# Rows of q and k loaded in three pieces, with gaps in the row buffers

## The chip, the core and the metric

The kernel runs on one core of a Trainium2 chip. The core has five engines that run their own instruction streams and wait for each other on semaphores: TensorE (matmuls, with its weight loads shown apart), VectorE (DVE), ScalarE (ACT), GpSimd (POOL) and SyncE (SP). Sixteen DMA engines move data between the chip's main memory and the two on-chip memories' buffer side (SBUF); matmul results go to eight PSUM banks of 128 x 512 float32. The metric is the device time of one execution in microseconds (us), as a median over runs. Lower is better.

## What is computed

Attention over 64 heads (8 batches of 8), each with 576 rows of 64 values, followed by a feed-forward layer. Each head's output is the sum of a coarse attention, over means of four rows, and a local attention, over rows at most three apart:

```python
q_d = q.reshape(B, H, Sd, factor, D).mean(axis=3)
...
out_d = sm_attn(q_d, k_d, v_d)
out_up = np.repeat(out_d, factor, axis=2)
mask = np.abs(pos[:, None] - pos[None, :]) < factor
...
out_local = np.matmul(attn, v)
return (out_up + out_local).astype(np.float32)
...
h = x @ w_in
g = h * (1.0 / (1.0 + np.exp(-h)))
return (g @ w_out).astype(np.float32)
```

`x` has one row for each of the 4608 positions and 512 columns (8 heads of 64); `w_in` is 512 x 2048, `w_out` 2048 x 512.

## The kernel before

The heads are handled as 32 pairs. One pair's q is a block of memory of 2 x 576 x 64 float32; the kernel reads it as 128 rows of 576 contiguous values, one row to a partition (9 positions of 64 values each). The same holds for k, whose blocks are read 64 rows further on, so that one k block serves two pairs in halves.

For pair 0, q and k come as float32 through the queues of SP and ACT, and VectorE and ScalarE convert them to bf16 into the buffer `qkb` (L753, L759). For pairs 1 to 31, POOL issues two DMAs a pair (q and k, L686; the issue itself is recorded at L676 or L740) that convert float32 to bf16 on the way and write `qkb` directly. `qkb` has six buffers of 128 x 2 x 576 bf16; a buffer is free again when TensorE has transposed what is in it and the next pair's half. These DMAs all go through one queue, q0, in the order in which POOL issues them. The eight blocks of the weights, `w_in` and `w_out`, go through the same queue, in between (L740, 512 pieces of 2048 B read for each block). The rows of v go through SP's queue, q1, in packets of 256 B (`vs`) and of 1024 B (`vq`), the outputs in packets of 2048 B.

TensorE transposes each pair's q and k in 36 small steps: a step takes 64 partitions and 64 values of a row (`pe_T`, L802, instructions at L810). The results are copied to `qT` and `kT`, from which the scores are formed (L571, "PS<-qT,kT"); exponentials, sums and products with v follow, and POOL's add at L1018 writes the result of a pair, transposed, into `xT`. Four pairs make one batch's 576 positions. The feed-forward layer runs in nine super blocks of 512 positions: 16 groups of four matmuls "PS<-xT,w_in_sb" each, ScalarE and VectorE in between, and then 16 matmuls "PS<-w_out_bf,gT" for each of four output tiles. Super block j can start only when the adds of all pairs that it covers are done: super block 0 needs pairs 0 to 3, super block 1 pairs 4 to 7 too, and so on. Until TensorE has such work it fills gaps with dummy matmuls on a constant ("PS<-dz").

The order of all instructions on every engine is fixed when the program is built, by a planner (class `Plan`, L253) that steps through a model of the engines with the cost written beside each job. The costs of the loads (0.87 and 0.57, `gran=0.106`, L688) are not touched by the change, so the order that comes out is the same instruction by instruction on all five engines; only line numbers and the shapes of the changed operands differ. POOL runs its stream strictly in order: row DMAs, weight DMAs, conversions of v (L565, "vb<-vs"), sums over four rows of v (L785, L790), and the adds (L1018).

The branch in `casts` that would convert a pair's q and k on POOL (L771) is never taken here, since the set `SW` holds all pairs from 1 to 31.

Of the kernel before, what the change touches and what calls it, by code (L numbers as in the profile page):

```python
# [6 lines left out]
AF = mybir.ActivationFunctionType  # L7
# [3 lines left out]
BF16 = mybir.dt.bfloat16  # L11
# [37 lines left out]
def D(p, left):  # L49
    return (22 + 1.5 * (p - 3) if p < 4 else 42 + 3 * (p - 7) if p < 8 else 45 + 8 * (p - 7)) - left  # L50
# [37 lines left out]
def HOLD(p):  # L88
    return ["S3"] if p == 4 else []
# [405 lines left out]
def bass_hourglass_attn__then__act_silu_kernel(  # L495
# [9 lines left out]
    with kctx:  # L505
        E = kctx.enter_context
        L = Plan()
        P = Prog()
        J = L.job
        res = {}  # L510

        def R(name, psum=False):
            if name not in res:
                res[name] = Res(name, psum)
            return res[name]

        def sb(name, shape, dt, n=None):
            if n is None:
                return E(nc.sbuf_tensor(name, shape, dt))
            return [E(nc.sbuf_tensor(f"{name}{i}", shape, dt)) for i in range(n)]  # L520
# [10 lines left out]
        vs = sb("vs", [128, 10, 64], F32, N_VS)  # L531
        vq = sb("vq", [128, 4, 256], F32, N_VQ)
        vt = sb("vt", [128, 4, 128], F32)
        qkb = sb("qkb", [128, 2, 576], BF16, N_QKB)
        vb = sb("vb", [128, 10, 64], BF16, N_VB)
        vd = sb("vd", [128, 4, 64], BF16, N_VD)
        qT = sb("qT", [128, S_], BF16, N_T)
# [26 lines left out]
        def copy(eng, e, out_, in_):  # L564
            return e.activation(out_, in_, AF.Copy) if eng == "ACT" else e.tensor_copy(out_, in_)  # L565

        def half(j):
            return slice(64 * j, 64 * j + 64)
# [102 lines left out]
        def rows(t, p, n, off):  # L671
            return bass.AP(tensor=t.tensor, offset=t.offset + (128 * p + off) * 576, ap=[[576, n], [1, 576]])

        def dma(name, eng, out_, in_, r, w, sem, work, cost, hold=(), **kw):
            def emit(j):
                P.op(j.ran, lambda s: s.dma_start(out_(), in_()), r() if r else [], w(), sem(), after=gates(hold))  # L676
            kw["pre"] = list(kw.get("pre", ())) + list(hold)
            J(name, eng, cost, emit, work=work, **kw)

        def loads(p, order):  # L680
            if p == 0:
                dma("lkx", LD_ENG("kx", 0), lambda: kx[64:128, :], lambda: rows(k, 0, 64, 0), None, lambda: rkx, lambda: "kx",
                    0.45, 0.43, due=order["kx"], take=[("qkb", -1)])
            for x, (t, n, off) in enumerate(((q, 128, 0), (k, 128 if p < NPAIR - 1 else 64, 64))):
                if p in SW:
                    dma(f"c{'qk'[x]}{p}", "POOL", lambda x=x, n=n: qkb[S("qkb", p)][0:n, x, :],  # L686
                        lambda t=t, n=n, off=off: rows(t, p, n, off), None, lambda x=x: [R(f"qkb{S('qkb', p)}{x}")],
                        lambda x=x: f"qkb{S('qkb', p)}{x}", 0.87, 0.57, gran=0.106, take=[("qkb", p)], due=-60 + p if p < 4 else D(p, 26.0),  # L688
                        hold=order.get(("gate", p), ()))
                    continue  # L690
                dma(f"l{'qk'[x]}{p}", LD_ENG("qk"[x], p), lambda x=x, n=n: qk[S("qk", p)][0:n, x, :],
                    lambda t=t, n=n, off=off: rows(t, p, n, off), None, lambda x=x: [R(f"qk{S('qk', p)}{x}")],
                    lambda x=x: f"qk{S('qk', p)}{x}", 0.85 * n / 128, 0.43, take=[("qk", p)] + ([("qkb", 0)] if p == 0 else []), due=order["qk", p],
                    hold=order.get(("gate", p), ()))
            for h in range(2):
                for j in range(2):
                    def emit(jb, h=h, j=j):
                        s = S("vs", p)
                        sem, w = f"vs{s}{h}{j}", [R(f"vs{s}{h}{j}")]
                        base = v[(2 * p + h) // H_, (2 * p + h) % H_]  # L700
                        T_, o = base.tensor, base.offset + (288 * j - 3) * D_
                        d, lo, hi = vs[s][half(j), 5 * h:5 * h + 5, :], 0, 5
                        if (p, h, j) == (0, 0, 0):
                            lo = 1
                            P.op(jb.ran, lambda e: e.dma_start(vs[s][3:64, 0, :], bass.AP(
                                tensor=T_, offset=base.offset, ap=[[64, 61], [1, 64]])), [], w, sem, after=gates(["vz"] + list(order.get(("gate", p), ()))))
                        if (p, h, j) == (NPAIR - 1, 1, 1):
                            hi = 4
                            P.op(jb.ran, lambda e: e.dma_start(vs[s][64:123, 9, :], bass.AP(
                                tensor=T_, offset=base.offset + 517 * D_, ap=[[64, 59], [1, 64]])), [], w, sem)  # L710
                        P.op(jb.ran, lambda e: e.dma_start(d[:, lo:hi, :], bass.AP(
                            tensor=T_, offset=o + 58 * 64 * lo, ap=[[64, 64], [58 * 64, hi - lo], [1, 64]])), [], w, sem,
                            after=gates(order.get(("gate", p), ())))
                    J(f"lv{p}{h}{j}", LD_ENG("v", p), 0.64, emit, work=0.39, gran=0.018, take=[("vs", p)],
                      due=order["v", p], pre=list(order.get(("gate", p), ())) + (["vz"] if p == 0 else []))
            if p >= VP_PE:
                def emit(jb):
                    i = S("vq", p)
                    base = v[2 * p // H_, 2 * p % H_]
                    T_, o = base.tensor, base.offset  # L720
                    P.op("SP", lambda e: e.dma_start(vq[i][:, 0:4:2, :], bass.AP(
                        tensor=T_, offset=o, ap=[[256, 128], [S_ * D_, 2], [1, 256]])), [], [R(f"vqm{i}")], f"vq{i}")
                    for j in range(2):
                        P.op("SP", lambda e, j=j: e.dma_start(vq[i][64 * j:64 * j + 16, 1:4:2, :], bass.AP(
                            tensor=T_, offset=o + 128 * 256, ap=[[256, 16], [S_ * D_, 2], [1, 256]])),
                            [R(f"vqc{i}1"), R(f"vqc{i}3")], [R(f"vqe{i}{j}")], f"vqe{i}{j}")
                J(f"lvq{p}", "SP", 1.6, emit, work=0.85, gran=0.046, take=[("vq", p)], due=order["vq", p],
                  pre=list(order.get(("gate", p), ())) + [f"vqz{(p - VP_PE) % N_VQ}"])
# [18 lines left out]
        def casts(p):  # L747
# [2 lines left out]

            def one(x):
                def emit(jb):
                    P.op(jb.ran, lambda e, a=i(), b=j(): copy(jb.ran, e, qkb[b][:, x, :], qk[a][:, x, :]),  # L753
                         [R(f"qk{i()}{x}")], [R(f"qkb{j()}{x}")])
                return emit

            if p == 0:
                def emit(jb):
                    P.op("ACT", lambda e, b=S("qkb", -1): e.activation(qkb[b][64:128, 1, :], kx[64:128, :], AF.Copy),  # L759
                         rkx, [R(f"qkb{S('qkb', -1)}1")])  # L760
                J("ckx", "ACT", 0.65, emit, pre=["lkx"], take=[("qkb", -1)], due=D(0, 9.4))
            use = dict(take=[("qkb", p)], use=[("qk", p)])
            if p in SW:
                pass
            elif p < CAST2:
                for x in range(2):
                    eng = C_ENG[p][x]
                    J(f"c{'qk'[x]}{p}", eng, {"DVE": 0.5, "ACT": 0.65, "POOL": 0.6}, one(x), pre=[f"l{'qk'[x]}{p}"],
                      port=True, due=D(p, 9.3), **use)
            else:  # L770
                def emit(jb):  # L771
                    P.op("POOL", lambda e, a=i(), b=j(): e.tensor_copy(qkb[b][:, :, :], qk[a][:, :, :]),
                         [R(f"qk{i()}0"), R(f"qk{i()}1")], [R(f"qkb{j()}0"), R(f"qkb{j()}1")])
                J(f"cq{p}", "POOL", 1.15, emit, pre=[f"lq{p}", f"lk{p}"] + HOLD(p), port=True, due=D(p, 10.3), marks={f"ck{p}": 1.0}, **use)

            def emitv(jb):
                a, b = S("vs", p), S("vb", p)
# [24 lines left out]
        def pe_T(p):  # L802
            a, b = S("qkb", p), S("qkb", p - 1)
            tiles = ((0, 0, 0, a), (0, 1, 1, a), (1, 1, 0, a), (1, 0, 1, b))
            for r in range(9):
                for j, h, x, n in tiles:
                    t, c = t_home(p, x, r)
                    o = PS[half(h), t, c:c + 32].bitcast(BF16)
                    w = qkb[n][half(j), x, 64 * r:64 * r + 64]
                    P.op("PE", lambda e, o=o, w=w, j=j: e.transpose(o, w, idn[half(j), :]),  # L810
                         [R("idn"), R(f"qkb{n}{x}")], [rB[t]])

# [484 lines left out]
```

## Time and profile before

| | |
|---|---|
| median of three runs | 341.86 us (341.33 to 343.66) |
| the profiled execution | 342.31 us, of which the span from first to last instruction is 340.5 us |
| granted TensorE clock over the span | 0.97 |
| busy: TensorE, VectorE, ScalarE, POOL | 96%, 67%, 53%, 46% |
| DMA queue q0 (POOL's): packets, share of 16 engines over the span | 13088, 26.2% |
| DMA queue q1 (SP's): packets, share | 56378, 30.8% |
| row DMAs into `qkb` from q: count, median from issue to landing | 31, 5.0 us |
| row DMAs into `qkb` from k: count, median from issue to landing | 30 of 128 rows, 5.4 us, and one of 64 |

The profile is one execution. The span is cut into 40 slices of about 8.5 us; this is TensorE's busy share, its granted clock and the DMA engines' busy share in each, in tenths:

```profile
PE   5587999999999999999999999999999999999996
...
PEclk9755999999999999999999999999999999999999
DMA  8997879999878976996398339500100010000112
```

The first four slices differ from the rest: TensorE is not full there and its clock is partly at half speed, while the DMA engines are busy. From the fifth slice on TensorE is full, and the DMA engines stay busy until about the 26th.

A duration in the profile is that of the recorded instruction or packet. TensorE's matmuls overlap, so sums of their durations exceed the time that passes. A packet's time includes waiting beside packets of other queues, so the shares of the queues can add up to more than 1. "issue" in the chain of waits is time in which an engine waited for nothing that the profile shows.

### The profile page before, as it was taken

How to read it: one execution, taken by the hardware profiler on the slowest of the kernel's cores; microseconds unless marked ns; L12 is line 12 of the kernel's file. 1: busy time of each engine (PE TensorE's matmuls, PEld its weight loads, DVE VectorE, ACT ScalarE, POOL GpSimd, SP SyncE). 2: the span in 40 equal slices, each digit the busy share in tenths (PEclk: the TensorE clock that was granted, in tenths of full speed). 3: DMA queues.
4: the chain of work that ended last, by engine and by line, in shares of the span. 5: the costliest groups of instructions: out<-in, count | busy, mean ns of one | idle time of the engine just before them, and what ended most of it. 6: DMA issues, size and time to landing. Idle time of an engine off the chain costs nothing.

```text
span 340.5 us, 10780 instructions
## 1 busy us (share of the span) xinstructions
PE 326.8 (96%) x4623; PEld 213.9 (63%) x4623; DVE 229.6 (67%) x410; ACT 179.0 (53%) x317; POOL 156.6 (46%) x211
## 2 busy tenths in 40 slices
PE   5587999999999999999999999999999999999996
PEld 2465677865555775587557755785577558866544
DVE  6586989866667885788577857796767556754200
ACT  5542756665544765476447645664656416644221
POOL 7363498435679667970698068704400140000000
PEclk9755999999999999999999999999999999999999
DMA  8997879999878976996398339500100010000112
GB/s 168 175 252 156 255 181 212 198 229 234 172 178 195 213 177 151 209 202 174 76 240 180 81 57 249 115 1 33 66 31 2 33 64 31 2 1 31 62 64 92
DMA packets 70666, 44.59 MB, mean 131 GB/s; under 512 B 45914, under 2 KB 63770, under 8 KB 70618
## 3 DMA queue, kind: packets, MB, share of 16 engines
q1 hardware_dynamic: 56378, 28.00, 30.8%
q0 software_dynamic: 13088, 15.36, 26.2%
q8 instruction: 36, 0.59, 0.7%
q10 hardware_dynamic: 1152, 0.54, 0.7%
q14 instruction: 12, 0.10, 0.1%
HBM read 45.61 MB, written 9.44 MB: 162 GB/s over the span
## 4 chain that ended last, share of the span: by engine, by line
PE 92%; DMA 2%; DVE 2%; issue 2%; POOL 1%; ACT 0%; POOLq 0%
PE PS L571 89%; PE PS L810 3%; DMA qkb<-in_k_dram 2%; DVE Pt L899 1%; POOL qkb L676 0%; DVE qd L845 0%; POOL gT L601 0%; DVE Rb L974 0%; DVE qT L565 0%; DVE kd L845 0%; DVE zt L964 0%; DVE zr L968 0%; ACT osb L1076 0%; DVE vd L565 0%; POOL idw L610 0%
## 5 line engine op out<-in xcount | busy, mean ns | idle before, releaser
L571 PE MATMUL PS<-xT,w_in_sb 128*128 128x512 f32 x576 | 141.2, 399 | 0.0
L571 PE MATMUL PS<-w_out_bf,gT 128*128 128x512 bf16 (+1 forms) x592 | 131.3, 374 | 0.0
L571 PEld LDWEIGHTS PS<-xT,w_in_sb 128*128 128x128 f32 x576 | 106.7, 188 | 24.7 <-DVE gT L1047 0.7
L1047 DVE SCALAR_TENSOR_TENSOR gT<-th,PS 128x512 bf16<-128x512 f32 x144 | 96.9, 683 | 37.0 <-ACT th L1043 36.3
L1043 ACT ACTIVATE th<-PS 128x512 f32<-128x512 f32 x144 | 86.1, 599 | 54.2 <-PE PS L571 46.0
L571 PEld LDWEIGHTS PS<-w_out_bf,gT 128*128 128x128 bf16 x592 | 54.7, 98 | 62.9 <-issue 3.5
L1018 POOL TENSOR_TENSOR xT<-xo 128x576 fp32r<-128x576 f32 (+5 forms) x48 | 43.5, 919 | 51.5 <-DVE xo L990 51.4
L565 POOL CAST vb<-vs 128x640 bf16<-128x640 f32 x32 | 24.4, 767 | 57.3 <-PE PS L571 42.5
L1100 ACT ACTIVATE osb<-PS 128x512 f32<-128x512 f32 x35 | 21.1, 603 | 53.6 <-PE PS L571 53.6
L893 ACT ACTIVATE Pt<-PS 128x576 bf16<-128x576 f32 x32 | 20.8, 649 | 33.0 <-PE PS L571 32.8
L785 POOL TENSOR_TENSOR vt<-vq 128x512 f32<-128x512 f32 x24 | 30.8, 1285 | 10.0 <-DMA vq<-in_v_dram 9.9
L990 DVE TENSOR_TENSOR xo<-PS,Rb 128x720 f32<-128x720 f32 x32 | 28.6, 893 | 5.1 <-PE PS L571 4.9
L974 DVE STREAM_TRANSPOSE Rb<-zr 128x768 f32<-128x768 f32 x32 | 30.9, 964 | 0.1
L899 DVE TENSOR_TENSOR Pt<-Pt,mask 128x576 bf16<-128x576 bf16 x24 | 16.3, 677 | 20.9 <-ACT Pt L893 20.9
L565 ACT ACTIVATE qT<-PS 128x576 bf16<-128x576 bf16 x30 | 19.8, 659 | 9.4 <-PE PS L810 9.4
L810 PE MATMUL PS<-idn,qkb 64*64 64x64 bf16 x1152 | 17.5, 201 | 7.5 <-issue 3.9
L845 DVE TENSOR_REDUCE qd<-qT 128x144 bf16<-128x576 bf16 x32 | 22.9, 716 | 1.5 <-ACT qT L565 1.4
L845 DVE TENSOR_REDUCE kd<-kT 128x144 bf16<-128x576 bf16 x32 | 23.0, 718 | 0.0
L964 DVE STREAM_TRANSPOSE zt<-PS 128x96 f32<-128x96 f32 x32 | 8.8, 274 | 20.2 <-PE PS L571 20.2
L565 ACT ACTIVATE kT<-PS 128x576 bf16<-128x576 bf16 x30 | 20.0, 665 | 1.6 <-PE PS L810 1.6
L810 PEld LDWEIGHTS PS<-idn,qkb 64*64 64x64 bf16 x1152 | 14.2, 115 | 9.5 <-issue 4.5
L676 POOL DMA_DIRECT2D qkb<-in_k_dram x31 | 17.1, 553 | 5.1 <-PE PS L810 5.1
(56 smaller groups left out, 229.3 us busy)
## 6 DMA issues: line engine op xcount, KB each, us to landing
vs<-in_v_dram SPq DMA_DIRECT2D x123, 80.0 KB, 4.6
out_dram<-osb SPq DMA_DIRECT2D x35, 256.0 KB, 3.6
vq<-in_v_dram SPq DMA_DIRECT2D x24, 256.0 KB, 4.3
qkb<-in_q_dram POOLq DMA_DIRECT2D x31, 144.0 KB, 5.0
qkb<-in_k_dram POOLq DMA_DIRECT2D x30, 144.0 KB, 5.4
w_in_sb<-in_moe_w_in_dram POOLq DMA_DIRECT2D x4, 1024.0 KB, 7.4
w_out_bf<-in_moe_w_out_dram POOLq DMA_DIRECT2D x4, 512.0 KB, 14.3
vq<-in_v_dram SPq DMA_DIRECT2D x48, 32.0 KB, 3.9
```

The source lines that it names most:

```text
L565: return e.activation(out_, in_, AF.Copy) if eng == "ACT" else e.tensor_copy(out_, in_)
L571: P.op("PE", lambda t: t.matmul(out_, lhsT, rhs, start=start, stop=stop, skip_group_check=True), r, w)
L785: P.op("POOL", lambda g: g.tensor_tensor(vt[:, :, :], vq[n][:, :, 0:128], vq[n][:, :, 128:256], ALU.add), [R(f"vqm{n}"), R(f"vqe{n}0"), R( ...
L810: P.op("PE", lambda e, o=o, w=w, j=j: e.transpose(o, w, idn[half(j), :]), [R("idn"), R(f"qkb{n}{x}")], [rB[t]])
L845: P.op("DVE", lambda e: e.tensor_reduce(dst, src.rearrange("p (g r) -> p g r", r=4), AX.X, ALU.add), [R(f"{'qk'[x]}T{s}")], [R(f"{'qk'[x]} ...
L893: P.op("ACT", lambda e: e.activation(d[:, :, :], PS[:, b[0]:b[1] + 1, a:e_], AF.Exp, scale=sc), [rB[b[0]], rB[b[1]]], [R(f"P{m}" if local ...
L974: P.op("DVE", lambda e: e.transpose(Rb[n][:, :].rearrange("p (c q) -> p c q", q=32), zr[z][:, :].unsqueeze(2).to_broadcast([128, 24, 32])) ...
L990: P.op("DVE", lambda e: e.tensor_tensor(xo[x][:, :, :], PS[:, bb[0]:bb[1] + 1, 0:360], Rb[u][:, :].rearrange("p (x c) -> p x c", x=2)[:, : ...
L1018: P.op("POOL", lambda g, dst=dst, in0=in0, in1=in1: g.tensor_tensor(dst, in0, in1, ALU.add), [R(f"xo{x}")], xblk(kc, t + a, t + e_))
L1043: P.op("ACT", lambda e: e.activation(th[x][:, :], PS[:, b, :], AF.Tanh, scale=0.5), [rB[b]], [R(f"th{x}")])
L1047: P.op("DVE", lambda e: e.scalar_tensor_tensor(gT[j % 2][:, f, :], th[x][:, :], 1.0, PS[:, b, :], ALU.add, ALU.mult), [rB[b], R(f"th{x}")] ...
L1100: P.op("ACT", lambda e, s=S("osb", n), b=bank(key)[0]: e.activation(osb[s][:, :], PS[:, b, :], AF.Copy, scale=0.5), [rB[bank(key)[0]]], [R ...
```

## The change

Each row of 576 values becomes three pieces of 192 in the buffer, with 8 unused values after each piece: `qkb` goes from 128 x 2 x 576 to 128 x 2 x 3 x 200 bf16, so a piece of 384 B starts every 400 B where a row of 1152 B was contiguous. The DMAs of pairs 1 to 31 get a three-level pattern on both sides (n rows, 3 pieces, 192 values); in main memory the pieces of a row still follow each other without a gap. The conversions of pair 0 read and write the same three-level pattern. The transposes read the same 64 values at their new place; 192 is three times 64, so no step crosses a piece's end. The branch that is never taken is removed. Nothing else changes; all later buffers in SBUF move by 576 B.

```diff
-        qkb = sb("qkb", [128, 2, 576], BF16, N_QKB)
+        qkb = sb("qkb", [128, 2, 3, 200], BF16, N_QKB)
...
+        def rows_3(t, p, n, off):
+            return bass.AP(tensor=t.tensor, offset=t.offset + (128 * p + off) * 576, ap=[[576, n], [192, 3], [1, 192]])
+
+        def parts(x):
+            return x.rearrange("p (a b) -> p a b", a=3)
...
-                    dma(f"c{'qk'[x]}{p}", "POOL", lambda x=x, n=n: qkb[S("qkb", p)][0:n, x, :],
-                        lambda t=t, n=n, off=off: rows(t, p, n, off), None, lambda x=x: [R(f"qkb{S('qkb', p)}{x}")],
+                    dma(f"c{'qk'[x]}{p}", "POOL", lambda x=x, n=n: qkb[S("qkb", p)][0:n, x, :, 0:192],
+                        lambda t=t, n=n, off=off: rows_3(t, p, n, off), None, lambda x=x: [R(f"qkb{S('qkb', p)}{x}")],
...
-                    P.op(jb.ran, lambda e, a=i(), b=j(): copy(jb.ran, e, qkb[b][:, x, :], qk[a][:, x, :]),
+                    P.op(jb.ran, lambda e, a=i(), b=j(): copy(jb.ran, e, qkb[b][:, x, :, 0:192], parts(qk[a][:, x, :])),
...
-                    P.op("ACT", lambda e, b=S("qkb", -1): e.activation(qkb[b][64:128, 1, :], kx[64:128, :], AF.Copy),
+                    P.op("ACT", lambda e, b=S("qkb", -1): e.activation(qkb[b][64:128, 1, :, 0:192], parts(kx[64:128, :]), AF.Copy),
...
-                    w = qkb[n][half(j), x, 64 * r:64 * r + 64]
+                    w = qkb[n][half(j), x, r // 3, 64 * (r % 3):64 * (r % 3) + 64]
```

More of the change, by code (lines that the diff above doesn't have):

```diff
@@ L769, in casts @@
                       port=True, due=D(p, 9.3), **use)
[L770 to L774, printed above, removed]
             def emitv(jb):
```

## The prediction

> **What bounds the kernel now.** First the page: busy times, and the chain that ended last.
>
> ```profile
> PE 326.8 (96%) x4623; PEld 213.9 (63%) x4623; DVE 229.6 (67%) x410; ACT 179.0 (53%) x317; POOL 156.6 (46%) x211
> ...
> PE 92%; DMA 2%; DVE 2%; issue 2%; POOL 1%; ACT 0%; POOLq 0%
> ```
>
> TensorE is the bound: a cost counts only where it makes TensorE wait. The chain in order of time says where that is (start, length, what):
>
> ```profile
> 2.13 1.69 POOL qkb L676 x3
> 3.82 7.52 DMA qkb<-in_k_dram
> ...
> 14.56 2.00 issue
> ...
> 20.82 1.12 issue
> ...
> 26.48 1.92 issue
> ...
> 36.39 20.78 PE PS L571 x304
> ```
>
> Before 36 us the chain hangs on the k rows of pair 2 (issued at 3.82, all landed at 11.34) and then on three stalls called issue. In each of these one 16 KB packet of the instruction queue is fetched: the trace has such packets starting at 13.96, 19.61 and 26.14, and TensorE goes on at 16.56, 21.94 and 28.40, 256 of its instructions apart. Each fetch starts only once TensorE is past the block before, so whatever delays pair 2 delays all that follows. From 36 us on TensorE hardly waits.
>
> Next the DMA queues, where they are full (q0 is POOL's, with the q and k rows; q1 is SP's, here with v packets of 256 B; last figure: share of 16 engines). From 64.5 to 66 us:
>
> ```profile
> q0 software_dynamic: 241, 0.24, 92.5%
> q1 hardware_dynamic: 241, 0.06, 29.6%
> ```
>
> The two queues take turns, packet by packet, 241 against 241. From 9 to 11 us:
>
> ```profile
> q0 software_dynamic: 307, 0.32, 91.7%
> q1 hardware_dynamic: 312, 0.08, 28.1%
> ```
>
> And from 29 to 34 us, v packets alone:
>
> ```profile
> q1 hardware_dynamic: 2232, 0.54, 49.0%
> ```
>
> **Price of a piece.** A v packet of 256 B took 0.490 x 5 us x 16 / 2232 = 17.6 ns. A row (2304 B read, 1152 B written, with the cast): 0.32 MB are 278 packets of 1152 B, the other 29 are tiny (some 0.4 us), so (0.917 x 2 x 16 - 0.4) / 278 = 104 ns. Output packets of 2048 B, from 280 to 330 us, took 86 ns (8.4% of 50 x 16 us, less 1 us for 96 small ones, over 768). The line through 256 and 2048 B gives 96 ns for 2304 B, so the cast adds about 8, and 37 for 768 B. A piece is 768 B read and 384 B written. Lower end 35 ns (a third of a row), upper end 104 (a piece costs as much as a row); I take 37 + 8 = 45, as 768 B lies between two points of the line. The v row matters here: at 256 B it lies on the same line as 2048 B, so smallness alone costs nothing beyond the 8 ns that every packet pays.
>
> The Trainium skill (DMA: Bandwidth & Descriptors, Specifications) puts the least size for line rate at 512 B and says that below it the engine reads, modifies and writes back. The v packets do not bear that out for aligned loads; no row of this trace shows pieces at a pitch of 400 B. That rule is the first rival below.
>
> **The start.** A transfer is 128 rows, 8 on each engine. In turn with v packets it took 8 x (104 + 18) = 0.98 us (139 rows per us from 9 to 11 us gives 0.92). In pieces: 24 x (45 + 18) = 1.51, so +0.53. The k rows of pair 2 are the fourth transfer in q0: +2.1 us. Ends: +1.2 at 35 ns, +7.8 at 104. If the three pieces of a row kept one turn, 8 x (3 x 45 + 18) = 1.22, it would be +1.0. POOL must write 384 descriptors for 128. Its issues (busy, mean ns):
>
> ```profile
> L676 POOL DMA_DIRECT2D qkb<-in_q_dram x31 | 17.7, 569 | 0.0
> ...
> L740 POOL DMA_DIRECT2D w_in_sb<-in_moe_w_in_dram x4 | 3.1, 781 | 0.0
> ```
>
> The second issues 512 pieces (128 x 4), the first 128. By count, 256 more cost 0.15 us; the whole difference is 0.21 to 0.23, as w_in also has three levels. I take +0.20 an issue, ends 0 and 0.23. Only the first transfer's issue lies on the chain: +0.2. The transfers of pair 3 land later too (13.23 before, third after pair 2's: about +3.2), against transposes at 13.94 that move by 2.3, so they start about 0.2 late; that sits inside the 2.00 us fetch stall. Pairs 4 to 7 land 3.5 us or more ahead of use before, and POOL issues them after the v cast at 13.94, which waits for v: v now gets three turns for each row, so this cast comes earlier, not later. The three casts of pair 0 (ACT 681 and 682 ns, DVE 450) now see three runs of 192: the last ends at 7.25 and the next wait of TensorE ends at 8.25, later still afterwards; 0, and even doubled 0.
>
> **After 36 us.** 62 transfers at +0.3 to +0.5 us each fill the queue more but land early: the ninth pair's k rows are issued at 49.90, the longest landing before 60 us is 18.7 us, its transposes start at 75.16; four transfers longer is 2.1 us against a cover of at least 6.6. The last w_out block, issued at 52.87, stands behind six row transfers: 71.1 + 3.2 us, and its first matmul, at 76.4, has moved with the rest; its cover was 5.3. Were these covers gone, each would cost its excess once. POOL's issues are another matter, since they stand in its order ahead of the adds that make xT:
>
> ```profile
> 54.91 1.21 POOL L1018 TENSOR_TENSOR xT<-xo 128x576 fp32r<-128x576 f32 x1 [0.71 <-DVE xo L990]
> ...
> 58.21 1.22 POOL L1018 TENSOR_TENSOR xT<-xo 128x576 fp32r<-128x576 f32 x1 [0.49 <-DVE xo L990]
> ```
>
> Seven row issues stand between POOL's idle time before 42.99 and the first of these adds: 7 x 0.20 - 0.71 idle = 0.69 late. Three more before the second: 0.69 + 0.60 - 0.49 = 0.8. That add ends at 59.42 and the first matmul of super block 1 starts at 59.44, so TensorE loses 0.8. In the two cycles before super block 3 (idle 0.31 and 0.22 against 0.40 each) 0.3 is left, of which the 0.22 us between the add's end and the matmul cover most: 0.1. Other blocks have idle 0.36 to 0.53 in every cycle. Sum +0.9; ends 0, and 1.3 at 0.23.
>
> The transposes read the same 64 values from other addresses: 35 in 0.31 us on the chain, 8.6 ns each. The nearest row with uneven addresses is q by k, 20 matmuls of 58 values in 0.18 us, 9.0 each, per value 15% more. So 0 to 32 x 0.05 = 1.6 us; I take 0, the shapes differ.
>
> **The clock.** Granted share in two stretches (column before the DMA share):
>
> ```profile
> 33.90:34.90 1.00, 1.00 (x11) 0.28 (x3) 1.00 (x3) 0.96 (x3) 1.00 (x2) 0.50 0.57 134
> 35.00:36.00 1.00, 1.00 (x57) 0.80 (x60) 1.00 (x4) 0.64 (x2) 1.00 (x2) 1.00 0.19 35
> ```
>
> It changes at 11.0, 14.4, 17.9 and 34.9, multiples of 3.4 us apart, and work that moves by 2.3 us meets other steps. The next is 38.3: up to 3.4 us at half speed, so 0 to +1.7; as 34.9 plus the shift lies 1.1 short of 38.3, half of that, +0.6.
>
> **Sum.** 2.1 + 0.2 + 0.9 + 0.6 = 3.8. The profiled execution took 342.31 us (span 340.5 and 1.8 around it), 0.45 above the median of 341.86, so 341.86 + 3.8 = 345.7.
>
> **Rivals.** *Small writes are dear*: a piece costs a row's 104 ns, decided where pieces are written. For it: pieces start 400 B apart, as nothing does now. Against it: 17.6 ns at 256 B. 7.8 + 0.2 + 0.9 + 0.6 = 9.5: 351.4. The w_out block would land near 82.8, still before its use at 85 or so. 0.15.
> *Half price*: the row is read whole and only the writes are split, or a row keeps one turn, or pieces cost 35: 1.1 + 0.2 + 0.3 = 1.6: 343.5. This takes in that the change hardly does what it says; it can't vanish, as the gap of 16 B keeps the writes apart. 0.15.
> *Not slower*: shorter packets let the instruction packet in sooner. It started 3.0 and 4.2 us after TensorE went on (16.56, 21.94), but 2.0 after 28.40, with the DMA share down from 1.2 to 0.59; if the wait falls to 2.0 beside pieces, the stalls of 1.12 and 1.92 shrink by 1.0 and 1.9, and the first by 0.5: 345.7 - 3.4 = 342.3. It decides once a turn's length, not the number of turns, sets that wait. Against it: more turns are queued. 0.10, a third of it with a clock step won as well, 1% faster.
> *Forecast*: 0.60, its own range 344 to 348.5.
>
> **Numbers.** 1% is 3.4 us, about what a measurement of this kernel can tell from no change: 338.4 and 345.3. Slower: 0.15 and 0.8 of the forecast's 0.60, 0.63. Faster: 0.04. Within: 0.33. The range goes down to 342.5, into the third rival, and up to 353, past the first: about 0.1 out on either side.
>
> **What would show it.** Right: some 23,600 row packets in q0 at about 45 ns; k rows of pair 2 landing near 13.6 and the three fetch stalls 2 to 3 us later, about as long; POOL issues near 0.75 us; super block 1 starting 3 us or more later; no new wait of TensorE on qkb after 36 us. Wrong: transfers landing as before, pieces near 104 ns, transposes slower than 0.31 us for 35, or w_out waits near 76 us.

## The result, and the profile after

| | median of n runs | shortest to longest |
|---|---|---|
| before | 341.83 us (14) | 340.05 to 343.66 |
| changed | 344.84 us (14) | 342.23 to 348.66 |

The ratio is 1.0088, with a 95% interval of 1.0068 to 1.0109: 3.0 us slower, just within the 1% that the prediction took as its bound. The spread has grown as well, from 3.6 to 6.4 us. The first profiled execution of the changed kernel happened to be the longest of its 14, so the lines below are from a second profile of the same kernel (347.28 us, span 345.4), which shows the same long wait near 147 us.

From its page: the busy times, the queues (packets, MB, share of 16 engines), and the chain that ended last.

```profile
PE 324.2 (94%) x4588; PEld 215.2 (62%) x4623; DVE 231.9 (67%) x410; ACT 179.0 (52%) x317; POOL 170.2 (49%) x211
...
q1 hardware_dynamic: 56378, 28.00, 32.0%
q0 software_dynamic: 28832, 15.36, 31.0%
...
PE 84%; POOL 6%; issue 4%; DVE 3%; DMA 2%; ACT 1%; POOLq 0%
```

q0 moves its bytes in 28832 packets where it had 13088, and POOL is busy 13.6 us longer. The share of TensorE in the chain, 84% in place of 92%, has to be read with care: in the first profile of the changed kernel it is 91%. Here TensorE waited once, 0.6 us, for an add of POOL that ended at 62.30, and the chain is followed back from there through POOL's unbroken work to 44 us, though TensorE was busy for 17.7 of the 18 us from 44 to 62. The chain in order of time, up to 38 us (start, length, what):

```profile
2.13 2.41 POOL qkb L682 x3
4.54 7.57 DMA qkb<-in_k_dram
...
15.52 1.36 issue
...
21.97 1.66 issue
...
27.83 2.80 issue
...
37.50 0.31 PE PS L812 x35
```

The k rows of pair 2 have landed at 12.11 instead of 11.34. The three stalls are still there: 1.36, 1.66 and 2.80 us, for 2.00, 1.12 and 1.92 before. The transposes cost what they did, 35 in 0.31 us.

The second loss is far from the loads. The chain from 136 to 152 us, cut to the stretch that matters:

```profile
143.87 3.86 DVE Pt L901
147.73 0.89 DVE Rb L976
148.62 0.63 DVE qd L847
149.25 0.67 DVE kd L847
```

L901 is VectorE's product of the exponentials `Pt` with the mask, a step that normally takes 0.39 or 0.46 us. Here one takes 3.86 us of the chain; `kd`, a mean over four rows of k that stands behind it on VectorE, comes late, and TensorE waits 2.7 us for it. What came next shows in two windows (window, length, busy us of PE, PEld, DVE, ACT and POOL with counts, granted clock, DMA share, GB/s):

```profile
149.90:153.40 3.50, 3.43 (x88) 2.99 (x89) 2.05 (x5) 1.61 (x3) 1.92 (x3) 0.51 1.31 264
146.50:149.90 3.40, 0.81 (x23) 0.33 (x21) 3.40 (x5) 0.90 (x2) 2.75 (x3) 1.00 1.11 292
```

TensorE was busy for 0.81 of 3.40 us, and in the next 3.5 us its granted clock was 0.51, which leaves some 1.7 us of work undone (3.5 x 0.49, an estimate). With the wait that is 4.4 us, about what was lost there: from the first matmul of super block 3 to that of super block 4 the changed kernel took 38.5 us (38.6 in the first profile), and 34.3 before.

### The profile page after: what moved, and what is told of

It reads as the page before. It is cut to its first block, busy times and chain, and to the rows that moved or that the text cites. A ratio compares the mean times of both kernels' runs of the same rounds, so it can differ in the third digit from the quotient of the medians.

```text
span 346.8 us, 10780 instructions
## 1 busy us (share of the span) xinstructions
PE 328.0 (95%) x4623; PEld 215.0 (62%) x4623; DVE 231.5 (67%) x410; ACT 178.9 (52%) x317; POOL 169.7 (49%) x211
## 3 DMA queue, kind: packets, MB, share of 16 engines
q0 software_dynamic: 28832, 15.36, 30.9%
q10 hardware_dynamic: 1152, 0.54, 0.7%
## 4 chain that ended last, share of the span: by engine, by line
PE 91%; issue 2%; DVE 2%; DMA 2%; POOL 1%; ACT 1%; POOLq 0%
PE PS L571 87%; PE PS L812 3%; DMA qkb<-in_k_dram 2%; DVE Pt L901 1%; POOL qkb L682 1%; ACT Pt L895 0%; POOL gT L601 0%; DVE Rb L976 0%; DVE xo L992 0%; DVE kd L847 0%; ACT qT L565 0%; DVE qd L847 0%; DVE vd L565 0%; ACT Pd L895 0%; ACT osb L1078 0%
## 5 line engine op out<-in xcount | busy, mean ns | idle before, releaser
L1049 DVE SCALAR_TENSOR_TENSOR gT<-th,PS 128x512 bf16<-128x512 f32 x144 | 97.0, 683 | 38.6 <-ACT th L1045 38.0
L901 DVE TENSOR_TENSOR Pt<-Pt,mask 128x576 bf16<-128x576 bf16 x24 | 17.8, 743 | 21.8 <-ACT Pt L895 21.8
L682 POOL DMA_DIRECT2D qkb<-in_k_dram x31 | 23.9, 770 | 12.6 <-PE PS L812 12.6
L565 ACT ACTIVATE qT<-PS 128x576 bf16<-128x576 bf16 x30 | 19.8, 660 | 11.1 <-PE PS L812 11.1
L682 POOL DMA_DIRECT2D qkb<-in_q_dram x31 | 24.2, 781 | 0.0
```

The costliest lines, as they stand in the source:

```text
L901: P.op(jb.ran, lambda e: e.tensor_tensor(Pt[m][:, :, :], Pt[m][:, :, :], mask[:, :].unsqueeze(1).to_broadcast([128, 2, 288]), ALU.mult), [ ...
L1049: P.op("DVE", lambda e: e.scalar_tensor_tensor(gT[j % 2][:, f, :], th[x][:, :], 1.0, PS[:, b, :], ALU.add, ALU.mult), [rB[b], R(f"th{x}")] ...
```

## The experiments

Each experiment was timed beside runs of the kernel before on the same chip; ratios are to those, with the 95% interval. All compute the whole result. Edits are shown against the kernel before unless another is named. In a kernel where only some pairs are in pieces, a row has a pitch of 600 values, and whole rows use the first 576; `hole` gives the one or the other, and the transposes' offsets follow.

**1. The changed kernel again.**

> The changed kernel once more, for a second profile. Theory START (the first 36 us are lengthened: later k rows and longer instruction-fetch stalls) expects the first matmul on w_in near 38.4 us against 36.3 before, and little more lost after it: total 344 to 345.5. Theory POOL (62 issues of 0.22 us more fill POOL, so adds and mask products come late) expects 1 us or more of the loss after that matmul, as new waits of TensorE on VectorE between 56 and 220 us.

Measured: 346.6 us (6 runs, 344.34 to 347.46), 1.0140 (1.0104 to 1.0175). The two intervals for the same kernel only just meet: the loss is not one number. Both theories have their sign in the trace: the first w_in matmul at 37.75, and the wait of 2.7 us on VectorE near 147 us.

**2. Pieces for pairs 0 to 7 alone, and 3. for pairs 8 to 31 alone.**

```diff
-                    dma(..., lambda x=x, n=n: qkb[S("qkb", p)][0:n, x, :],
-                        lambda t=t, n=n, off=off: rows(t, p, n, off), ...
+                    dma(..., lambda x=x, n=n: hole(S("qkb", p), 0, n, x, IN3(p)),
+                        lambda t=t, n=n, off=off: (rows_3 if IN3(p) else rows)(t, p, n, off), ...
...
+def IN3(p):
+    return p < 8        # experiment 3: p >= 8
```

> Pieces for pairs 0 to 7 only, whole rows for pairs 8 to 31 (same buffers of 600 values per row). START expects nearly the whole loss: 344 to 345, first matmul on w_in near 38.4 us. POOL expects little: under 0.8 us over before.

> Pieces for pairs 8 to 31 only, whole rows for pairs 0 to 7. START expects 341.8 to 342.5, first matmul on w_in at 36.3 us as before. POOL expects 1.5 to 3 us over before, with adds into xT late before super blocks 1 and 3 and mask products held up.

Early pieces: 344.69 us, 1.0077 (1.0048 to 1.0105). Late pieces: 341.44 us, 0.9996 (0.9971 to 1.0021), though two of its 12 runs (344.46 and 345.88) lie above all 27 runs of before beside it (at most 343.30). So the steady loss is in the first eight pairs, and the 48 later transfers cost nothing in the median, but stretch the spread.

In the chains the three stalls called issue are 1.85, 1.39 and 2.75 us with early pieces, and 2.92, 1.89 and 1.92 with late ones. A single stall varies too much to compare (2.92, since TensorE reached that one earlier). What compares better is when TensorE begins each stretch of 256 instructions, as read from the records (good to some 0.1 us), and its first feed-forward matmul:

| profiled execution | second stretch | fifth stretch | first w_in matmul |
|---|---|---|---|
| before | 11.46 | 28.43 | 36.32 |
| late pieces (3) | 10.66 | 28.59 | 36.36 |
| changed, first and second profile | 11.97, 12.24 | 30.98, 30.67 | 38.45, 37.75 |
| early pieces (2) | 11.91 | 30.72 | 38.49 |
| mean of six with whole rows early | 10.97 | 28.5 | 36.2 |
| mean of six with pieces early | 12.13 | 31.1 | 38.6 |

The six of each kind are before, 3, 4, 8, 9 and 11, and the two profiles of the changed kernel, 2, 7, 10 and 12. Pieces make the second stretch begin 1.2 us later, when the k rows have landed, and the three fetches after it take 1.4 us more between them (18.4 to 19.1 us from the second stretch to the fifth, against 15.6 to 18.6). Nothing is added from there to the first matmul. That is 2.4 us; the medians of experiment 2 differ by 3.1, and the other 0.7 is not accounted for. The larger buffers themselves cost nothing that shows: experiments 3 and 4 keep rows of 600 values and all later buffers where they are in the changed kernel, at 0.9996 and 1.0008.

**4. Whole rows, but POOL's time of the pieces.** A fill of a scratch tile goes ahead of each row issue.

```diff
+                if j.ran == "POOL":
+                    P.op("POOL", lambda g: g.memset(scr[:, :], 0.0), [R("scr")], [R("scr")])
                 P.op(j.ran, lambda s: s.dma_start(out_(), in_()), r() if r else [], w(), sem(), after=gates(hold))
```

> Whole rows for all pairs, and a fill of a 128 x 128 float32 scratch tile on POOL (some 0.22 us) before each of the 62 row issues: POOL's time without the packets. POOL expects the same loss as with pieces, 344 to 345. START with the packets as its cause expects under 1 us over before, and the three fetch stalls as before.

Measured: 341.82 us, 1.0008 (0.9991 to 1.0025). With a fill of 224 ns an issue and its fill took 0.71 us, less than the 0.78 of an issue in pieces, so this came out weaker than the thing it stood for. At this strength the loss that theory POOL expected isn't there. It is done again, larger, as experiment 9.

**5. Pieces for pairs 1 to 3 alone, and 6. for pairs 4 to 7 alone.** As experiment 2, with `1 <= p < 4` and `4 <= p < 8`.

> Pieces for pairs 1 to 3 only, the six transfers ahead of everything else. If the loss at the start is the later k rows of pair 2 (theory LANDING), it is here: first matmul on w_in 0.5 to 1 us later, total +0.5 to +1 us. If it is the instruction fetches beside the pieces of pairs 4 to 7 (theory FETCH), little is lost here beyond 0.5 us, and the second and third fetch intervals stay at 5.4 to 6.5 us.

> Pieces for pairs 4 to 7 only. FETCH: TensorE's second and third instruction blocks arrive 6.3 to 7.3 us after the ones before, against 5.4 to 6.5, the first matmul on w_in is 1.2 to 1.8 us later, and so is the end. LANDING: nothing is lost, since these rows land 3.5 us or more before their use.

Measured: 343.69 us, 1.0062 (1.0038 to 1.0087), and 343.45 us, 1.0056 (1.0032 to 1.0081). Neither theory has these numbers. Pairs 1 to 3 alone cost about 2.5 us, where LANDING gave them 0.5 to 1 and FETCH at most 0.5; pairs 4 to 7 alone cost 2.2, where LANDING gave them nothing. By the medians each half costs nearly as much as the eight pairs together (1.0077), but the intervals are too wide to tell whether the two costs add.

The profiled execution of 5 was its shortest, 341.44, and shows no loss (first w_in matmul at 36.17): its k rows of pair 2 landed at 12.32, as late as with all the pieces, but its three fetches took 16.6 us, as with whole rows. So a later landing alone didn't cost this execution anything, and what the others of its kind lost is not in a trace. That of 6 is 1.5 us late (37.77), but not where FETCH put it: the second and third blocks came 5.1 and 6.5 us after the ones before, no later than with whole rows. The fourth fetch started 4.9 us after TensorE had gone on, for 2.0 in the kernel before, and the one after the first w_in matmul 5.0. That pieces for pairs 4 to 7, whose rows land well ahead of use, cost anything speaks for the instruction fetch, since those transfers hold up nothing else that the trace shows; but that is argued from one execution. Whether it is the number of packets ahead of the fetch or their total time was not separated.

**7 and 8. The mask in float32**, in the changed kernel and in the kernel before, meant to change how VectorE reads the product's operands.

```diff
-        mask = sb("mask", [128, 288], BF16)
+        mask = sb("mask", [128, 288], F32)
```

> The changed kernel with the mask kept in float32, so that VectorE's product with it no longer runs in the faster two-byte form. Theory PORT (a product of 0.46 us that falls into an unbroken run of POOL work is held up to 3.9 us, and the pieces' longer issues make such runs) expects no product over 1 us, no stall of TensorE on VectorE near 146 us, and a total 1.5 to 3 us under the changed kernel's. If the long products only mirror a wait that lies elsewhere, the total stays at 344.8 to 346.6.

> The kernel before with the mask in float32. Its own held products are 2.5, 1.6 and 1.3 us; one of 2.5 us at 81.4 us costs TensorE about 0.6 us. PORT expects 340.5 to 341.5, no product over 1 us. The other view, that the plain form's 0.2 us more for each of 24 products costs as much as it saves, expects no change or up to 0.5 us more.

Measured: 348.85 us, 1.0210 (1.0183 to 1.0237), and 341.95 us, 1.0025 (1.0008 to 1.0041). As a remedy this failed, and PORT's expectation with it in both kernels: the product itself takes 0.3 us longer (median 760 ns for 459), and it is still held, 2.84 us at the longest in experiment 8. The loss there, 0.7 us, is about what the other view expected. The view of the product's line in experiment 7 (minimum, median and maximum in ns):

```profile
L901 DVE TENSOR_TENSOR Pt<-Pt,mask x24: 695/760/3949, 79.4 to 284.7; 128x576 bf16<-128x576 bf16 x24
```

In its profiled execution, its longest (354.28), three products took 3.85, 3.95 and 3.95 us, and TensorE waited 5.9 us for `kd` in three places.

**9. Whole rows with a larger fill**, 128 x 192 for 128 x 128, so that issue and fill together take the 0.78 us of an issue in pieces.

> Whole rows, with a larger fill (128 x 192 float32) before each row issue, so that issue and fill take 0.78 us together, as an issue of pieces does; in e4 it was 0.71. Theory TURN (POOL's cycle of 5.75 us has so little slack that 0.46 us more makes a mask product lose its turn near 138 us, which delays the next adds by 1.3 us and puts the following product behind an unbroken run of POOL work) expects held products of 1.9 and 3.9 us before super block 3 in at least some executions, and a median 1 to 4 us over before. If POOL's time is harmless and the pieces themselves hold the products, the median stays within 0.5 us of before, as in e4.

Measured: 342.28 us, 1.0023 (0.9996 to 1.0049). Seven of its runs lie between 341.2 and 342.4 and five between 343.4 and 346.9, all five above the longest of the 23 runs of before beside it (343.25). Two lines of VectorE's timeline (start, length, engine, line, operation):

```profile
111.41 3.56 DVE L914 TENSOR_TENSOR Pt<-Pt,mask 128x576 bf16<-128x576 bf16 x1
...
143.37 2.71 DVE L914 TENSOR_TENSOR Pt<-Pt,mask 128x576 bf16<-128x576 bf16 x1
```

The median, 0.7 us over before, is less than TURN gave and more than its rival. But the long products are here without any pieces: more time on POOL, with whole rows, is enough for them, and the spread of the runs suggests that they come in some executions and not in others.

**10 and 11. In turn.** In the changed kernel (10) and the kernel before (11), POOL's casts of v, its sums and its adds wait for the last mask product that the plan puts ahead of them. Nothing else is changed.

```diff
-                P.op(jb.ran, lambda e: e.tensor_tensor(
+                lastk[0] = P.op(jb.ran, lambda e: e.tensor_tensor(
                     Pt[m][:, :, :], Pt[m]...
...
-                         [R("vt")], [R(f"vd{m}")])
+                         [R("vt")], [R(f"vd{m}")], after=lastk[0:1])
```

> The changed kernel, with each of POOL's casts, sums and adds made to wait for the mask product that the planner put ahead of it. TURN expects no product held over 2.6 us, super block 4 34 to 35 us after super block 3 instead of 38.5, and the loss of the start alone: 343 to 344.5. If the held products are not what lengthens the stretch after 137 us, the total stays at 344.8 to 346.6.

> The kernel before with the same waits. TURN expects the product at 81.4 us to take 0.5 us instead of 2.5 and the end 0 to 0.8 us earlier: 340.7 to 341.5. The other view, that POOL's waits cost it more than the product gains, expects 341.5 to 342.5.

Measured: 343.59 us, 1.0070 (1.0043 to 1.0097), six runs within 2.3 us; and 340.97 us, 0.9980 (0.9961 to 1.0000). The product's line in the changed kernel, in experiment 10 and in experiment 11, one view of each:

```profile
L901 DVE TENSOR_TENSOR Pt<-Pt,mask x24: 394/459/3940, 78.5 to 277.6; 128x576 bf16<-128x576 bf16 x24
```

```profile
L906 DVE TENSOR_TENSOR Pt<-Pt,mask x24: 394/459/1424, 79.2 to 274.9; 128x576 bf16<-128x576 bf16 x24
```

```profile
L904 DVE TENSOR_TENSOR Pt<-Pt,mask x24: 393/457/459, 75.8 to 271.7; 128x576 bf16<-128x576 bf16 x24
```

The longest falls from 3940 to 1424 ns, and in whole rows from 2542 to 459. Super block 4 begins 34.6 us after super block 3, as TURN expected, for 38.5. The profiled execution of 10 loses at the start alone (first w_in matmul at 38.85, 2.5 us late); by the medians the loss is 2.0 us. That the whole kernel gains by the waits is likely and not settled: its interval overlaps that of the changed kernel's 14 runs. Experiment 11 has the lowest median of all, but the end of its interval is 1.0000, so that it beats the kernel before is likely and not settled.

**12. A pitch of 416 B** in place of 400, in the changed kernel.

```diff
-        qkb = sb("qkb", [128, 2, 3, 200], BF16, N_QKB)
+        qkb = sb("qkb", [128, 2, 3, 208], BF16, N_QKB)
```

> The changed kernel with 16 unused values after each piece instead of 8, so that every piece starts at a multiple of 32 B (pitch 416 B for 400). If the odd pitch costs anything, a piece falls from 49 to 51 ns to some 45 and the loss at the start by a quarter. If only the number of pieces counts, packets and total stay as with 400 B: 344.8 to 346.6.

Measured: 344.4 us, 1.0082 (1.0055 to 1.0109), 0.4 under the range expected for no effect; its start lost as much as the others (first w_in matmul 2.7 us late). The pieces took the same: in the records of single packets the median is 51 ns at either pitch, and 106 for a whole row. So it is not where the pieces start that costs, at these two pitches.

## Why the products are held, and in which executions

Two timelines of the changed kernel, second profile. First VectorE's:

```profile
143.59 0.28 DVE L970 RECIPROCAL zr<-zt 128x24 f32<-128x24 f32 x1
143.79 3.94 DVE L901 TENSOR_TENSOR Pt<-Pt,mask 128x576 bf16<-128x576 bf16 x1
147.66 0.97 DVE L976 STREAM_TRANSPOSE Rb<-zr 128x768 f32<-128x768 f32 x1
```

and POOL's in that time:

```profile
143.62 0.71 POOL L565 CAST vb<-vs 128x640 bf16<-128x640 f32 x1
144.31 0.72 POOL L792 TENSOR_TENSOR vd<-vt 128x256 bf16<-128x256 f32 x1
144.99 1.48 POOL L1020 TENSOR_TENSOR xT<-xo 128x288 fp32r<-128x288 f32 x3
146.43 0.79 POOL L682 DMA_DIRECT2D qkb<-in_q_dram  x1
147.21 0.78 POOL L682 DMA_DIRECT2D qkb<-in_k_dram  x1
```

The product reads `Pt` and the mask, both in SBUF. POOL's cast, its sum and its adds read SBUF too, and follow each other without a gap. The product ends 0.5 us after the first row issue ends (147.22), its normal length, as if it had been held from 143.79 to there, through six of POOL's operations. In the kernel before the same product came at 142.53, just after `vd` had ended (142.46), and took 0.40 us. There it was POOL's three adds that took longer, 1.79 us for 1.49 in the two cycles before (both engines in one view):

```profile
142.48 1.79 POOL L1018 TENSOR_TENSOR xT<-xo 128x288 fp32r<-128x288 f32 x3
142.53 0.40 DVE L899 TENSOR_TENSOR Pt<-Pt,mask 128x576 bf16<-128x576 bf16 x1
```

The Trainium skill (SBUF — State Buffer, section "Who interferes with whom") says that a VectorE instruction with two inputs in SBUF contends with a GpSimd instruction that reads SBUF, and not with one that only writes it; it calls the shared ports an exclusive lock, and says that the order of issue decides who blocks. The trace agrees in the main: the holds in all profiles lie over casts, sums and adds, and experiment 7 fits, since a float32 mask leaves two inputs in SBUF. In experiments 3 and 9 the products of over 2.7 us ended 0.3 us after the last cast or add (114.98 after 114.66, for one). But in both profiles of the changed kernel the product ended 1.26 us after the last add, and 0.5 us after the row issue that followed it. Why it was held through that issue, and why VectorE loses several turns in a row, no run here shows.

Which executions meet this depends on how POOL's cycle lies against VectorE's. In the second profile a product at 136.59 met POOL's sum `vt` and took 1.90 us; the adds after it came late (POOL idle 1.22 us), POOL's cycle slid, and with 0.78 us for each of two row issues ahead of the next cast it stood right across the next product. That more time on POOL for each issue can take its cycle across is what experiment 9 shows (0.78 us, holds of 3.56 and 2.71); the profile of 4 has nothing over 2.54 (0.71 us). It needn't happen: with issues of 0.78 us the profile of experiment 12 has nothing over 1.02. That issues of 0.55 us leave POOL the time to recover from such a slip is argued, not shown. The account over the profiled executions, each against that of before (342.31 us, first w_in matmul at 36.32):

| execution | time | lost by the first w_in matmul | lost after it | longest product |
|---|---|---|---|---|
| changed, first profile | 348.66 | +2.1 | +4.2 | 3.90 |
| changed, second (1) | 347.28 | +1.4 | +3.5 | 3.94 |
| early pieces (2) | 343.94 | +2.2 | -0.5 | 2.54 |
| late pieces (3) | 344.46 | 0.0 | +2.1 | 3.45 |
| POOL's time, 0.71 us (4) | 342.53 | +1.0 | -0.8 | 2.54 |
| pairs 1 to 3 (5) | 341.44 | -0.1 | -0.7 | 2.53 |
| pairs 4 to 7 (6) | 344.75 | +1.5 | +1.0 | 2.54 |
| pieces, float32 mask (7) | 354.28 | +2.7 | +9.2 | 3.95, 3.95, 3.85 |
| rows, float32 mask (8) | 342.37 | +0.6 | -0.5 | 2.84 |
| POOL's time, 0.78 us (9) | 344.20 | -1.9 | +3.8 | 3.56 |
| pieces, in turn (10) | 344.53 | +2.5 | -0.3 | 1.42 |
| rows, in turn (11) | 341.32 | -0.6 | -0.4 | 0.46 |
| pitch 416 B (12) | 344.35 | +2.7 | -0.7 | 1.02 |

Pieces in all of the first eight pairs lose 1.4 to 2.7 us by the first w_in matmul. After it, every execution with a product of 3.4 us or more loses 2.1 us or more, and of the others only experiment 6 loses anything, 1.0 us, before super block 1, where its fetches are late. The first profile of the changed kernel has a late fetch there too, a stall of 1.1 us at 47 us, which is in its 4.2. Before itself has a product of 2.54 us, at 81 us, and it cost something: TensorE waited 0.6 us for the `kd` behind it:

```profile
86.48 0.29 PE L571 MATMUL PS<-qd,kd 64*64 64x144 bf16 x8 [0.59 <-DVE kd L845]
```

## Why the prediction was right or wrong

The forecast of 345.7 was 0.9 above the median, inside its own range of 344 to 348.5; but slower by over 1% was given 0.63, and the 0.88% is just short of it. That the sum came so near is in part luck. By the first w_in matmul 2.4 us were lost (mean of six) for 2.3 forecast, but of another make-up; the 0.9 for POOL's adds and the 0.6 for the clock are not there as a steady loss; and the held products, which some executions pay for with 2 to 4 us, were not forecast.

- **Price of a piece: right, a tenth low.** Predicted 45 ns. From 9 to 11 us in the changed kernel:

```profile
q0 software_dynamic: 629, 0.23, 93.9%
q1 hardware_dynamic: 547, 0.13, 48.6%
```

0.23 MB are 599 pieces of 384 B, and 30 packets are tiny: (0.939 x 2 x 16 - 0.4) / 599 = 49.5 ns. The rival "small writes are dear" (104 ns) is out: three pieces took 150 ns where a row took 104, far from three times as long. The Trainium skill (DMA: Bandwidth & Descriptors, Specifications) puts the least size for line rate at 512 B. In direction these pieces agree, with 7.8 B written in a ns for 11.1 in a row, but the price of a whole row for each is not borne out; whether anything was read back, no run shows. That the v packet "lies on the same line as 2048 B" was no evidence: the line was drawn through these two points.

- **The landing of the k rows, 2.1 + 0.2: nearly twice too much.** "24 x (45 + 18) = 1.51" added the two queues' times as if they excluded each other. The same window shows that they overlap: their shares sum to 143% (120% before), and 599 pieces in 2 us are 100 rows per us, 1.28 us a transfer in place of 0.92, so +0.36 and not +0.53. The fourth transfer landed at 12.0 on average in the six profiles with pieces early, and at 10.8 in the five with whole rows that have a record of it: +1.2 for 2.3, the issue included.
- **The fetch stalls, "about as long": wrong.** They grew by 1.4 us in all, which nearly made up for the missing 1.1. The rival "not slower" had them shrink. It asked the right question, what a fetch waits for behind a full queue, and gave the wrong sign; the point held against it, that more turns are queued, fits what came.
- **An issue, +0.20: right in size, smaller in effect.**

```profile
L682 POOL DMA_DIRECT2D qkb<-in_q_dram x31 | 24.3, 783 | 0.2 <-DMA w_in_sb<-in_moe_w_in_dram 0.2
L682 POOL DMA_DIRECT2D qkb<-in_k_dram x31 | 23.9, 772 | 9.6 <-PE PS L812 9.6
```

783 for 569 and 772 for 553 ns: +0.21 and +0.22. The 0.8 us before super block 1 failed in the step "that add ends at 59.42 and the first matmul of super block 1 starts at 59.44, so TensorE loses 0.8". In the second profile that add begins at 61.07, and the super block's first matmul had started at 60.88, as long after the first w_in matmul as before (23.1 us): two times that stood side by side were taken for a wait, so a super block can start before the last add of its pairs has ended, other than the text ahead of the prediction has it. A later matmul of the block did wait for the add, 0.6 us here, 0.3 in the profiles of experiments 3 and 12, none in the first profile; but super block 2 began only 0.14 us later against super block 1 than before. Experiments 4 and 9, which have POOL's time without the pieces, are 0.3 and 0.7 us over before in the median, not clear of nothing in either.
- **Before super block 3, 0.1: missed.** The slack that the prediction counted, idle time of POOL ahead of the adds, was there. It did not look at who else is held while POOL is busy: the lengthened issues move POOL's reads across VectorE's product, for nothing in some executions and some 4 us in others. In the trace of before, products of 2542, 1590 and 1335 ns beside a median of 458 were there to be seen, and so was TensorE's wait of 0.6 us behind the first of them.
- **The clock, +0.6: not seen at the start**, where fifth stretch to first matmul took 7.7 us on average with rows and 7.55 with pieces. It halved at 150 us instead, after the 2.7 us wait.
- **After 36 us, 0 for the transfers and the transposes: right.** No wait of TensorE on `qkb`, the transposes at 0.31 us for 35 (8.9 ns each, not 8.6, which changes nothing), late pieces at 0.9996. The casts of pair 0, also put at 0, were right too: VectorE's took 742 ns for 450 with three runs of 192, but ended only 0.1 us later, and ScalarE's took what they did.

"Half price" (343.5) came nearly as close as the forecast, 1.3 below the median, and had the start nearly right, 1.1 + 0.2; it too lacked the fetches and the products. The range, 342.5 to 353, held the median, and 13 of 14 runs.

## What to carry to other kernels

Splitting a DMA's rows can cost in three places, and only the first stands in the transfer's own duration: the packets, the issuing engine's time for the descriptors, and whatever waits beside the packets in other queues, here most likely the instruction fetches. Before adding time to an engine whose slack looks sufficient, list the instructions of one kind whose longest duration is several times their median, and see which engine's work lies over them: a longer step there can move a harmless hold onto the path. A spread that grows with a change is a finding of its own, and two ends of instructions that coincide in one trace are not a dependency until a wait says so.

## What the runs showed of the hardware

- A piece of 384 B (768 B read, converted) took 51 ns and a row three times as long 106; a pitch of 400 or 416 B made no difference.
- 256 more descriptors made an issue on POOL 0.22 us longer.
- TensorE's next 256 instructions came 4.6 to 7.0 us after the block before in the second profile, with both data queues full, though the packet that brings them lasts only about 1 us: most of it is the delay until that packet starts, 2.1, 4.2 and 4.8 us there against 2.5, 3.0 and 4.2 before.
- A product of 0.46 us on VectorE took up to 3.94 us while POOL ran operations that read SBUF and a row issue after them; with POOL made to wait its turn the longest was 0.46 in whole rows, and the 24 products together took 10.4 us instead of 16.3.
